# Block-causal attention and two MLP layers on one core: another table for the planner, with part of the normalization on GpSimd

## The chip, the cores and the metric

One Trainium2 chip, one core. The metric is the device time of one execution in microseconds (us). Engines are named as the profile names them: PE (TensorE, with PEld for its weight loads), DVE (VectorE), ACT (ScalarE), POOL (GpSimd), SP (SyncE, which issues nearly all DMAs).

## The reference

```python
# q, k, v: 4 batches x 8 heads x 576 tokens x 64
scores = 0.125 * q @ k.T
scores = np.where(block_i >= block_j, scores, -1e9)   # blocks of 64 tokens
attn = np.exp(scores - max(scores)); attn /= attn.sum(-1) + 1e-9
x = (attn @ v)                                        # as 2304 x 512
h = x @ w_in                                          # 512 x 2048
x = (s * np.maximum(h, 0)**2 + b) @ w_out             # 2048 x 512
h = max(x @ w1, x @ w2, x @ w3)                       # 512 x 768 each
out = h @ w_out2                                      # 768 x 512
```

The weights (`moe_w_in`, `moe_w_out`, `moe2_w*`) reach the kernel as pairs of 32-bit words and are taken apart on the chip.

## The kernel before, in words

Every product of the MLP layers is made of three fp32r matmuls on 128 rows and 128 columns (high by high, high by low, low by high part), so each operand exists as a high and a low part that ACT, DVE or POOL makes. Attention goes through 16 pairs of heads (`p` = 0 to 15). For a pair there are nine score units: units 1 to 8 cover 128 queries of one head each (192, 320, 448 or 576 keys; `unit`, line 573) and unit 0 the first 64 queries of both heads (`first`, line 546). DVE takes the row maximum out of PSUM (`most`, line 531), ACT the exponential with its row sum (`expo`, line 536). PE then transposes the exponentials in five groups a to e (`turned`, line 669), ACT or DVE copies them out, and PE multiplies them by the values (`product` A to E, line 672). The sums become reciprocals once a batch (four pairs), are turned, written to DRAM and read back over 64 partitions, and `normalize` (line 847) multiplies the result in `xf` by them, chunk by chunk (five chunks of 512 or 384 tokens); `split_x` (line 870) then makes high and low part of a chunk. The first three chunks go through the first half of the first MLP layer plainly, all that is left by Strassen's scheme with seven products. `convert` (line 745) makes float32 weights from those words.

PE works in three shapes. Scores and MLP use the array as one tile of 128 rows and 128 columns. The products A to E use two tiles of 128 rows and 64 columns side by side, one for each head (`side`), in plain fp32, for which the profile records two matmuls for each one in the code. Unit 0 also stands side by side, but contracts over 64 rows only, that is with tiles of 64 rows and 64 columns: two matmuls of 64 columns in the code, four records. `side_by_side` (line 698) collects what has been put on the list `side` and issues it as one block of PE work, in the order in which it was put there.

The order on every engine is computed when the program is built. Operations are recorded with the engines allowed, a cost in ns, what they read and write, and a due time (place in the recording plus `CFG['off']` of their kind); `Sched.run` (line 201) then fills the engines' in-order queues in model time. It holds POOL and those DVE operations that are marked `lock` to one at a time (`port`), and charges PE for going into and out of side-by-side blocks (line 261). It charges nothing for what stands inside such a block. 60 filler matmuls (kind `warm`, line 1142, 128x256) take PE's free places at the start. In what order the parts of a pair are recorded is a string:

```python
        for x in CFG["order%d" % p if p < 2 else "order"]:   # line 1248
```

A digit records that score unit (0 puts `first` on the list `side`), a small letter turns that group of the pair before, a capital puts that product of the pair before on `side`, `p` prepares the next pair's operands and loads those after, `v` loads values, and `|` issues the list as one block. Before, the string was

```python
        'order': '20DaEbC6|p75AB41||vd|ce3||8',
```

so its first block holds unit 0, then D, E and C.

For each pair the operands are made from `raw` tiles: high parts of keys and queries (`khi`, `qhi`), their low parts (`klo`, line 377 by a helper, and the query's on DVE, line 499) and `k0` for unit 0; `CFG['eng']` (and `eng0`, `eng1` for pairs 0 and 1) says on which engines. Pair 0 uses plain fp32 scores (tile `xf`) with one scaling operation `q2` of the queries ahead.

Of the kernel before, what the change touches and what calls it, by code (L numbers as in the profile page):

```python
# [29 lines left out]
EPS = 1e-9  # L30

# [33 lines left out]
def c_dve(n):  # L65
    return n / 0.96 + 68
# [22 lines left out]
def c_pooltt(n):  # L89
    return 2.4 * n + 100  # L90
# [64 lines left out]
class Sched:  # L155
# [45 lines left out]
    def run(self):  # L201
        n = len(self.ops)
# [25 lines left out]
        while len(order) < n:  # L228
# [28 lines left out]
            if e == "PE":  # L257

                m = self.ops[i][5]
                if side != (m == "side"):  # L260
                    c += 92 if not side else 126 if m == "turn" else 256
                side = m == "side"
# [20 lines left out]
def tile_attention_moe(ctx: ExitStack, tc: tile.TileContext, qk, vp, w_in, w_out, ms_, b_, w123, w_out2, out):  # L283
# [98 lines left out]
    def load(size, f, eng="SP", after=(), lat=2000, **k):  # L382

        k["after"] = [op(eng, 380, f, lat=lat, after=after, **k)]
        return op("DMA", size / (CFG["rate"] if k.get("kind") in ("w", "w2", "wf") else 330), lambda e: None, lat=1000 + CFG["dm"].get(k.get("kind"), 0), **k)
# [37 lines left out]
    def load_pair(p):  # L423
# [3 lines left out]
        if p == 0:  # L427

            for i, e_ in enumerate(("SP", "ACT")):
                def f(e, i=i):  # L430
                    (nc.sync if i == 0 else nc.scalar).dma_start(out=R[i].ap[0:64, 0:2 * S], in_=qk[b, hp, 0:64, i])
                load(294912, f, e_, lat=1260, writes=[(R[i], k) for k in ALL])
        else:
            for i in range(2):
                def f(e, i=i):
                    nc.sync.dma_start(out=R[i].ap, in_=qk[b, hp, :, i])
                load(589824, f, lat=2000 if p < 3 else CFG["dlat"], writes=[(R[i], k) for k in ALL])
# [75 lines left out]
    def load_values(p):  # L513
# [5 lines left out]
        load(557056, f, lat=2000 if p < 2 else CFG["dlat"], writes=[V])  # L519
        return V  # L520

    def softmax_pair(p, P, DEN):
# [86 lines left out]
    def values_pair(p, E, V):  # L609
# [7 lines left out]
        def turn(groups, u):  # L617
# [3 lines left out]
            for g in groups:  # L621
# [11 lines left out]
                op({x: y(n) for x, y in (("ACT", c_act), ("DVE", c_dve)) if x in CFG["pe"]}, 0, f,  # L633
# [213 lines left out]
    def normalize(c):  # L847
# [4 lines left out]
        for k in range(KT):  # L852
# [12 lines left out]
            op(CFG_E("xn", DVE=c_dve(n), Pool=c_pooltt(n)), 0, f, reads=[N] + [(XF, (k, i, tok)) for i in bs for tok in (0, 64)],  # L865
# [4 lines left out]
    def split_x(c, ring="x1"):  # L870
        c0, n = CHUNKS[c]
        for k in range(KT):
# [10 lines left out]
            j = op(CFG_E("xlo", DVE=c_dve(n), Pool=c_pooltt(n)), 0, f, reads=[(XF, ("x", c, k)), (X, 0)], writes=[(X, 1)], kind="xs", lock=True)  # L883
# [547 lines left out]
    with tc.manual_schedule():  # L1431
        for t, i, e in order:
# [4 lines left out]
CFG = {'aside': (6, 9, 12, 14, 18, 19, 23),  # L1437
        'aside3': (1, 1, 1, 0, 0, 0, 2, 0, 0, 2, 2, 0, 1, 1, 0, 2),
        'dlat': 5000,
        'dm': {'w': 1500, 'w2': 3300, 'wf': 2400},  # L1440
        'duo': (),
        'e': [2, 2, 2, 2, 2],
        'eng': {'k0': ['Pool', 'ACT', 'DVE'], 'khi': ['DVE'], 'klo': ['DVE', 'Pool'], 'q2': ['DVE', 'ACT', 'Pool'], 'qhi': ['DVE', 'Pool']},
        'eng0': {'k0': ['Pool', 'ACT'], 'khi': ['Pool', 'ACT', 'DVE'], 'klo': ['DVE'], 'q2': ['ACT'], 'qhi': ['Pool', 'DVE']},
        'eng1': {'k0': ['DVE'], 'khi': ['Pool', 'DVE', 'ACT'], 'klo': ['Pool', 'DVE'], 'q2': ['Pool', 'ACT'], 'qhi': ['ACT', 'Pool']},
        'ew': {'aff': ['ACT'],
               'hhi': ['DVE'],
# [9 lines left out]
        'je': ['ACT', 'DVE'],  # L1457
# [3 lines left out]
        'off': {'av': 625,  # L1461
                'exp': -7725,
                'h': -1300,
                'hf': -4560,
                'jc': -3650,
                'l1': -60,
                'l2': 40,
                'max': -6825,
                'phi': -1350,
                'prep': 125,  # L1470
                'prep0': -1000,
                'prep2': -350,
                'prepk': -2100,
                'prepklo': -7450,
                'preplo': -825,
                'smm': 175,
                'tr': -4875,
                'u': 260,
                'w': 940,
                'w0': -450,  # L1480
                'w2': 820,
                'warm': 1000000,
                'wf': -4620,
                'x2': -1160,
                'xn': 1340,
                'xs': 960},
# [70 lines left out]
```

## Time and profile before

| | |
|---|---|
| median of 3 runs | 822.62 us (822.43 to 823.08) |
| the profiled execution | 822.2 us |
| its span, first to last instruction | 820.4 us |
| PE busy | 814.6 us, 99% of the span, 4898 matmul records |
| DVE busy | 616.7 us, 75%, 1347 instructions |
| ACT busy | 479.3 us, 58%, 1100 instructions |
| POOL busy | 64.6 us, 8%, 57 instructions |
| granted TensorE clock, mean of the core | 1.000 |

Busy times of PE are modelled from the starts of its matmuls, so that a busy PE is not yet one at its peak: how fast it goes is read from how many matmuls start in a stretch. DVE and ACT have their load in attention (the first 160 us), where they are above 90% busy; later they have room.

### The profile page before, as it was taken

The numbers are of one execution on the slowest core, as the hardware profiler recorded it, in microseconds if no ns is written. First come the engines' busy times: TensorE is split into PE (matmuls) and PEld (weight loads), VectorE is DVE, ScalarE is ACT, GpSimd is POOL, SyncE is SP. The second block draws the span as 40 slices with busy tenths as digits, with TensorE's granted clock in tenths as the row PEclk, the third lists the DMA queues.
The fourth block names the chain that finished last, engine by engine and source line by source line (L and its number), as shares of the span: only waits on it lengthen the run. The fifth ranks groups of instructions, "written<-read, shape, count | busy, mean of one in ns | idle before, by whom it ended". The sixth has DMA issues, their size and how long they took to land. (4 is left out here: it accounts for less than half of the span.)

```text
span 820.4 us, 14499 instructions
## 1 busy us (share of the span) xinstructions
PE 814.6 (99%) x4898; PEld 741.4 (90%) x4898; DVE 616.7 (75%) x1347; ACT 479.3 (58%) x1100; POOL 64.6 (8%) x57
## 2 busy tenths in 40 slices
PE   9999999999999999999999999999999999999998
PEld 7778887878888899999999999999999899999996
DVE  7889999998778898879967997986557245833551
ACT  6888989986665688689666669622143122412111
POOL 5344254000000000000000000000000000000000
PEclk9999999999999999999999999999999999999999
DMA  7877786465678599899679799899676477666742
GB/s 236 256 253 210 230 275 208 177 192 198 228 262 305 211 302 354 307 353 376 203 271 323 259 319 338 291 306 306 212 232 206 142 228 229 181 194 188 225 128 77
DMA packets 92178, 200.77 MB, mean 245 GB/s; under 512 B 10948, under 2 KB 16452, under 8 KB 92100
## 3 DMA queue, kind: packets, MB, share of 16 engines
q1 hardware_dynamic: 91880, 199.41, 73.2%
q8 instruction: 39, 0.64, 0.3%
q10 hardware_dynamic: 224, 0.43, 0.2%
q14 instruction: 35, 0.29, 0.1%
HBM read 152.24 MB, written 43.85 MB: 239 GB/s over the span
## 5 line engine op out<-in xcount | busy, mean ns | idle before, releaser
L380 PE MATMUL ps<-arena 128*128 128x384 f32 (+4 forms) x3834 | 719.7, 347 | 1.4 <-DVE arena L1135 1.2
L380 PEld LDWEIGHTS ps<-arena 128*128 128x128 f32 x3834 | 668.9, 188 | 43.3 <-issue 1.4
L959 ACT ACTIVATE other<-ps 128x384 f32<-128x384 f32 x154 | 75.0, 487 | 186.8 <-PE ps L380 169.3
L954 DVE TENSOR_TENSOR other<-ps,other 128x384 f32<-128x384 f32 x129 | 71.2, 554 | 106.2 <-PE ps L380 90.0
L377 DVE TENSOR_TENSOR arena<-other,arena 128x384 fp32r<-128x384 f32 (+3 forms) x201 | 117.9, 598 | 5.2 <-ACT arena L364 2.3
L538 ACT ACTIVATE other<-ps,other 128x192 f32<-128x192 f32 (+4 forms) x144 | 77.7, 550 | 14.9 <-DVE other L533 14.5
L366 DVE TENSOR_SCALAR arena<-other 128x384 fp32r<-128x384 f32 (+3 forms) x148 | 60.2, 410 | 29.6 <-PE ps L380 19.7
L372 ACT ACTIVATE other<-ps 128x512 f32<-128x512 f32 (+1 forms) x102 | 55.8, 572 | 40.3 <-PE ps L380 36.2
L533 DVE TENSOR_REDUCE other<-ps 128x1 f32<-128x192 f32 (+4 forms) x144 | 66.9, 513 | 8.1 <-PE ps L380 7.3
L628 PEld LDWEIGHTS ps<-ident,other 128*128 128x128 f32 x400 | 43.9, 141 | 15.4 <-ACT other L538 10.7
L380 PE MATMUL ps<-other 128*64 128x64 f32 (+5 forms) x640 | 55.1, 313 | 0.0
L377 DVE TENSOR_TENSOR other<-other 128x256 fp32r<-128x256 f32 (+1 forms) x125 | 52.7, 433 | 1.6 <-ACT other L364 0.6
L760 ACT ACTIVATE other<-other 128x512 f32<-128x512 f32 x64 | 43.1, 676 | 17.8 <-DVE other L756 17.8
L628 PE MATMUL ps<-ident,other 128*128 128x128 f32 x400 | 53.4, 277 | 0.0
L768 DVE SCALAR_TENSOR_TENSOR other<-other 128x512 uint32<-128x512 uint32 x64 | 43.6, 687 | 6.7 <-ACT other L760 6.2
L364 ACT ACTIVATE other<-other 128x256 fp32r<-128x256 f32 (+2 forms) x95 | 39.0, 426 | 12.2 <-DMA bscr<-other 4.9
L1345 ACT ACTIVATE other<-other,cst 128x384 f32<-128x384 f32 x64 | 44.7, 701 | 0.7
L364 ACT ACTIVATE arena<-other 128x384 fp32r<-128x384 f32 (+1 forms) x66 | 36.4, 562 | 13.2 <-DVE other L377 10.2
L380 PEld LDWEIGHTS ps<-other 128*64 128x64 f32 (+1 forms) x640 | 26.9, 136 | 13.8 <-issue 9.7
L374 DVE COPY other<-ps 128x384 f32<-128x384 f32 (+2 forms) x49 | 28.2, 597 | 14.2 <-ACT other L372 11.9
L377 POOL TENSOR_TENSOR arena<-other,arena 64x1152 fp32r<-64x1152 f32 x11 | 37.8, 3436 | 11.9 <-PE ps L380 7.4
L1330 ACT ACTIVATE other<-other 128x384 f32<-128x384 f32 x48 | 24.8, 520 | 17.3 <-DVE other L954 17.2
(46 smaller groups left out, 426.7 us busy)
## 6 DMA issues: line engine op xcount, KB each, us to landing
arena<-bscr SPq DMA_DIRECT2D x301, 256.0 KB, 3.3
bscr<-other SPq DMA_DIRECT2D x119, 256.0 KB, 4.0
other<-qk SPq DMA_DIRECT2D x30, 576.0 KB, 5.1
other<-w_in SPq DMA_DIRECT2D x24, 512.0 KB, 5.0
other<-w_out SPq DMA_DIRECT2D x22, 512.0 KB, 5.4
other<-w SPq DMA_DIRECT2D x18, 512.0 KB, 6.1
other<-vp SPq DMA_DIRECT2D x16, 544.0 KB, 5.0
other<-pscr SPq DMA_DIRECT2D x24, 192.0 KB, 4.3
```

The lines of the kernel that those rows point to most:

```text
L364: nc.scalar.activation(out=dst, in_=src, func=AF.Copy, scale=m)
L366: nc.vector.tensor_scalar(out=dst, in0=src, scalar1=m, scalar2=None, op0=ALU.mult)
L372: nc.scalar.activation(out=dst, in_=src, func=AF.Copy)
L377: eng[e].tensor_tensor(out=dst, in0=a, in1=b, op=ALU.subtract)
L380: nc.tensor.matmul(o, l, r, start=start, stop=stop, **k)
L533: nc.vector.tensor_reduce(out=NM.ap[:, u:u + m], in_=v, axis=axis, op=ALU.max, negate=True)
L538: nc.scalar.activation(out=ev, in_=v, func=AF.Exp, bias=NM.ap[:, u:u + 1], scale=1.0, accum_out=DEN.ap[:, d:d + 1])
L628: nc.tensor.transpose(TB.ap[:, 128 * i:128 * i + 128], x, ident)
L768: nc.vector.scalar_tensor_tensor(out=lo_w, in0=hi_w, scalar=3, in1=lo_w, op0=ALU.logical_shift_left, op1=ALU.bitwise_or)
L954: nc.vector.tensor_tensor(out=out_.ap, in0=bank.ap[:, 0:HN], in1=u.ap, op=ALU.add)
L959: nc.scalar.activation(out=u.ap, in_=bank.ap[:, 0:HN], func=func)
L1345: nc.scalar.activation(out=u.ap, in_=u.ap, func=AF.Identity, scale=s_t, bias=b_t)
```

## The change

It changes numbers of the planner and its table, and where a few operations may run. In the planner: DVE's and ACT's copies of the transposes and the row maxima are charged 46 ns more (`EV`), two-operand work on POOL 2.7 instead of 2.4 ns a column, the ways into and out of side-by-side blocks 150, 216 and 290 instead of 92, 126 and 256 ns, loads of queries, keys and values other rates; weight loads are charged 1500 and 1600 ns less delay. In the kernel: the multiplications by the reciprocal sums of chunks 0 to 2 go to POOL, as does the low part of chunk 0 (`CFG['pool']`); the two units of 192 keys (i = 0) of a pair share a PSUM bank and one maximum (`duo`); high parts of hidden values may be made by ACT too; the result of a pair is copied out by DVE alone (`je`); `qhi` and `k0` go to ACT or POOL, `klo` to POOL. The strings and due times are others.

```diff
+EV = 46
 def c_pooltt(n):
-    return 2.4 * n + 100
+    return 2.7 * n + 100
...
-                    c += 92 if not side else 126 if m == "turn" else 256
+                    c += 150 if not side else 216 if m == "turn" else 290
...
-            op("DVE", c_dve(n), f, reads=reads, writes=[(NM, u + i) for i in range(m)], kind="max")
+            op("DVE", c_dve(n) + EV, f, reads=reads, writes=[(NM, u + i) for i in range(m)], kind="max")
...
-            op(CFG_E("xn", DVE=c_dve(n), Pool=c_pooltt(n)), 0, f, reads=[N] + [(XF, (k, i, tok)) for i in bs for tok in (0, 64)],
+            op({"Pool": c_pooltt(n)} if c < CFG["pool"][0] else CFG_E("xn", DVE=c_dve(n), Pool=c_pooltt(n)), 0, f, reads=[N] + [(XF, (k, i, tok)) for i in bs for tok in (0, 64)],
...
-            j = op(CFG_E("xlo", DVE=c_dve(n), Pool=c_pooltt(n)), 0, f, reads=[(XF, ("x", c, k)), (X, 0)], writes=[(X, 1)], kind="xs", lock=True)
+            j = op({"Pool": c_pooltt(n)} if c < CFG["pool"][1] else CFG_E("xlo", DVE=c_dve(n), Pool=c_pooltt(n)), 0, f,
+                   reads=[(XF, ("x", c, k)), (X, 0)], writes=[(X, 1)], kind="xs", lock=True)
...
-CFG = {'aside': (6, 9, 12, 14, 18, 19, 23),
-        'aside3': (1, 1, 1, 0, 0, 0, 2, 0, 0, 2, 2, 0, 1, 1, 0, 2),
+CFG = {'aside': (8, 11, 12, 14, 17, 18, 20),
+        'aside3': (2, 0, 0, 0, 1, 2, 0, 1, 3, 1, 0, 0, 0, 0, 0, 3),
-        'dm': {'w': 1500, 'w2': 3300, 'wf': 2400},
-        'duo': (),
+        'dm': {'w': 0, 'w2': 1700, 'wf': 2400},
+        'duo': (0,),
-        'eng': {'k0': ['Pool', 'ACT', 'DVE'], 'khi': ['DVE'], 'klo': ['DVE', 'Pool'], 'q2': ['DVE', 'ACT', 'Pool'], 'qhi': ['DVE', 'Pool']},
+        'eng': {'k0': ['ACT', 'Pool'], 'khi': ['DVE'], 'klo': ['Pool'], 'q2': ['Pool', 'DVE', 'ACT'], 'qhi': ['ACT', 'Pool']},
-        'eng0': {'k0': ['Pool', 'ACT'], 'khi': ['Pool', 'ACT', 'DVE'], 'klo': ['DVE'], 'q2': ['ACT'], 'qhi': ['Pool', 'DVE']},
+        'eng0': {'k0': ['Pool'], 'khi': ['ACT'], 'klo': ['Pool'], 'q2': ['DVE'], 'qhi': ['ACT']},
-               'hhi': ['DVE'],
+               'hhi': ['ACT', 'DVE'],
-        'je': ['ACT', 'DVE'],
+        'je': ['DVE'],
...
-        'order': '20DaEbC6|p75AB41||vd|ce3||8',
-        'order0': 'BpD3bc274Av5aC|6|8dE10e',
-        'order1': 'E0aA|D4618|bv5eCd||pB|c|3|72',
+        'order': 'CD20Ea|||vb6p74|5A1dB|e|||c3|8|',
+        'order0': 'p|av|EbC64e2cB37A|5|d81D0',
+        'order1': 'DaA2b0|p6||1B8||dE||5v7|e|c||C|3|4||',
+        'pool': (3, 1),
-        'pt': (1, 1, 2, 1, 1),
+        'pt': (1, 1, 1, 1, 1),
```

Where the changed kernel's instructions stand, at three places. First PE in one pair's cycle in the middle of attention: `arena` operands are scores, `ident,other` transposes, `other` alone the side-by-side products. Before:

```order
L380 MATMUL ps<-arena 128x320 x2
L380 MATMUL ps<-arena 128x288 x4
L380 MATMUL ps<-arena 128x192 x2
L380 MATMUL ps<-other 64x64 x2
L380 MATMUL ps<-other 64x128 x2
L380 MATMUL ps<-other 64x64 x10
L380 MATMUL ps<-other 64x256 x2
L628 MATMUL ps<-ident,other 128x128 x14
```

Now:

```order
L381 MATMUL ps<-arena 128x320 x2
L381 MATMUL ps<-arena 128x288 x4
L381 MATMUL ps<-arena 128x192 x4
L381 MATMUL ps<-other 64x256 x2
L381 MATMUL ps<-other 64x128 x2
L381 MATMUL ps<-other 64x64 x12
L629 MATMUL ps<-ident,other 128x128 x14
```

The block that holds unit 0 began with its two matmuls (64x64 x2). Now C (64x256) and D (64x128 and two of 64x64) come first, then unit 0 as the third and fourth of the twelve 64x64, then E. This follows from the string's `CD20E`, and is so for pairs 2 to 15. Over the whole program there are 33 side-by-side blocks before and now, with the same matmuls; 30 were followed by transposes and three by 128x128 matmuls, now 26 and seven; all 33 followed 128x128 matmuls, now 28 do and five follow transposes.

Second, PE at the start: `arena` 128x256 are the fillers, `xf` the scores of pair 0. Before:

```order
L380 MATMUL ps<-arena 128x256 x24
L380 MATMUL ps<-xf 128x192
L380 MATMUL ps<-arena 128x256 x5
L380 MATMUL ps<-xf 128x320
L380 MATMUL ps<-xf 128x288 x2
L380 MATMUL ps<-xf 128x320
L380 MATMUL ps<-xf 128x448 x2
L380 MATMUL ps<-xf 128x288 x2
L380 MATMUL ps<-xf 128x192
L380 MATMUL ps<-arena 128x256 x19
L628 MATMUL ps<-ident,other 128x128 x8
```

Now:

```order
L381 MATMUL ps<-arena 128x256 x29
L381 MATMUL ps<-xf 128x192 x2
L381 MATMUL ps<-xf 128x448
L381 MATMUL ps<-xf 128x320 x2
L381 MATMUL ps<-xf 128x288 x2
L381 MATMUL ps<-xf 128x448
L381 MATMUL ps<-xf 128x288 x2
L381 MATMUL ps<-arena 128x256 x14
L629 MATMUL ps<-ident,other 128x128 x14
L381 MATMUL ps<-arena 128x256 x17
L381 MATMUL ps<-other 64x64 x2
L381 MATMUL ps<-other 64x512 x2
```

The five fillers between the first and the second score matmul now stand ahead of the first, the scores run through, and 31 fillers follow them as before. The first side-by-side block holds unit 0 of pair 0, product A and, in the next row (64x64 x2), unit 0 of pair 1, where both units stood ahead of A. The 14 transposes are groups a and b of pair 0, and group a needs all eight exponentials.

Third, POOL in the later pairs, now: 64x1152 is `klo`, L865 the multiplication by the reciprocal sums, `arena<-xf` chunk 0's low part.

```order
L378 TENSOR_TENSOR arena<-other,arena 64x1152
L369 TENSOR_SCALAR other<-other 64x128
L865 TENSOR_TENSOR xf<-xf,other 128x512 x2
L378 TENSOR_TENSOR arena<-xf,arena 128x512
L378 TENSOR_TENSOR arena<-other,arena 64x1152
L378 TENSOR_TENSOR arena<-xf,arena 128x512
L865 TENSOR_TENSOR xf<-xf,other 128x512
L378 TENSOR_TENSOR arena<-other,arena 64x1152
```

Before, one `klo` of 64x1152 and one `qhi` of 128x1024 stood here for a pair, and none of the other rows; three of the 14 `klo` were on DVE. Now all 14 stand on POOL with 12 multiplications and four low parts between them, and three `qhi` are left.

## Rows read from the trace of the kernel before

**Rows 1.** The page: the span, and busy time by engine (share, instructions).
```profile
span 820.4 us, 14499 instructions
PE 814.6 (99%) x4898; PEld 741.4 (90%) x4898; DVE 616.7 (75%) x1347; ACT 479.3 (58%) x1100; POOL 64.6 (8%) x57
```
**Rows 2.** Who waited for whom, PE: us in total, times, longest.
```profile
PE ps L380 <- DVE arena L1135: 1.2, 1, 1.2
...
PE ps L380 <- DVE other L1415: 0.3, 1, 0.3
```
**Rows 3.** Stretches: length, then PE, PEld, DVE, ACT, POOL; clock, DMA, GB/s.
```profile
40.00:80.00 40.00, 40.00 (x361) 31.04 (x358) 36.20 (x69) 34.93 (x111) 16.97 (x12) 1.00 0.76 237
80.00:120.00 40.00, 40.00 (x385) 31.76 (x384) 38.93 (x71) 36.48 (x114) 15.41 (x14) 1.00 0.78 246
120.00:160.00 40.00, 40.00 (x362) 31.87 (x361) 39.20 (x82) 36.19 (x106) 13.01 (x7) 1.00 0.66 210
...
360.00:400.00 40.00, 40.00 (x232) 39.98 (x231) 37.44 (x87) 35.15 (x75) 0.00 (x0) 1.00 0.89 321
```
**Rows 4.** PE in order of time, one pair: start, length, engine, line, form, records.
```profile
62.17 1.72 PE L380 MATMUL ps<-other 64*64 64x64 f32 x32
63.82 1.75 PE L628 MATMUL ps<-ident,other 128*128 128x128 f32 x14
...
71.41 0.81 PE L380 MATMUL ps<-other 64*64 64x64 f32 x11
```
**Rows 5.** PE in order of time, the last pair's block of C, D and E.
```profile
154.73 1.45 PE L380 MATMUL ps<-other 128*64 128x128 f32 x28
156.11 2.95 PE L628 MATMUL ps<-ident,other 128*128 128x128 f32 x25
```
**Rows 6.** PE in order of time, 72 MLP matmuls behind a transpose, behind a block.
```profile
161.70 16.61 PE L380 MATMUL ps<-arena 128*128 128x512 f32 x72
...
179.89 16.66 PE L380 MATMUL ps<-arena 128*128 128x512 f32 x72
```
**Rows 7.** PE in order of time, the start.
```profile
1.18 4.44 PE L380 MATMUL ps<-arena 128*128 128x256 f32 x24 [1.18 <-DVE arena L1135]
6.34 0.56 PE L380 MATMUL ps<-xf 128*128 128x192 f32 x2 [0.71 <-issue]
6.60 0.89 PE L380 MATMUL ps<-arena 128*128 128x256 f32 x5
7.33 5.07 PE L380 MATMUL ps<-xf 128*128 128x320 f32 x18
12.10 2.56 PE L380 MATMUL ps<-arena 128*128 128x256 f32 x19
14.51 1.26 PE L628 MATMUL ps<-ident,other 128*128 128x128 f32 x8
```
**Rows 8.** ACT in order of time: scaling of queries, last exponential of pair 0.
```profile
5.82 0.42 ACT L364 ACTIVATE xf<-xf 64x256 f32<-64x256 f32 x1 [1.18 <-DMA xf<-qk]
...
14.85 0.20 ACT L538 ACTIVATION_READ_ACCUMULATOR other<-ps,other 128x1 f32 x1
```
**Rows 9.** POOL in order of time: two `klo` of the same size.
```profile
28.65 2.64 POOL L377 TENSOR_TENSOR arena<-other,arena 64x1152 fp32r<-64x1152 f32 x1 [3.47 <-DVE arena L366]
...
36.17 3.62 POOL L377 TENSOR_TENSOR arena<-other,arena 64x1152 fp32r<-64x1152 f32 x1 [1.04 <-DVE arena L366]
```
**Rows 10.** DVE in order of time, beside the second of them.
```profile
36.06 1.22 DVE L499 SCALAR_TENSOR_TENSOR arena<-other,arena 64x1024 fp32r<-64x1024 f32 x1
```
**Rows 11.** DVE groups by form: count, busy us, mean ns, idle before them.
```profile
L756 DVE TENSOR_SCALAR other<-other 128x512 f32<-128x512 f32 x64 | 27.0, 421 | 3.4 <-DMA other<-w_in 2.5 <-DMA other<-w_out 0.8
...
L864 DVE TENSOR_TENSOR xf<-xf,other 128x512 f32<-128x512 f32 x12 | 8.2, 685 | 0.1
L377 DVE TENSOR_TENSOR arena<-xf,arena 128x512 fp32r<-128x512 f32 x12 | 7.9, 677 | 0.1
...
L374 DVE COPY xf<-ps 128x512 f32<-128x512 f32 x3 | 2.1, 685 | 0.2 <-PE ps L380 0.2
...
L374 DVE COPY xf<-ps 128x64 f32<-128x64 f32 x3 | 0.6, 216 | 0.0
```

More of the change, by code (lines that the diff above doesn't have):

```diff
@@ L380, in mm, with load @@
         nc.tensor.matmul(o, l, r, start=start, stop=stop, **k)
-    def load(size, f, eng="SP", after=(), lat=2000, **k):
+    def load(size, f, eng="SP", after=(), lat=2000, rate=330, **k):
         k["after"] = [op(eng, 380, f, lat=lat, after=after, **k)]
-        return op("DMA", size / (CFG["rate"] if k.get("kind") in ("w", "w2", "wf") else 330), lambda e: None, lat=1000 + CFG["dm"].get(k.get("kind"), 0), **k)
+        return op("DMA", size / (CFG["rate"] if k.get("kind") in ("w", "w2", "wf") else rate), lambda e: None, lat=1000 + CFG["dm"].get(k.get("kind"), 0), **k)
     def CFG_E(k, **c):
@@ L431, in f @@
                     (nc.sync if i == 0 else nc.scalar).dma_start(out=R[i].ap[0:64, 0:2 * S], in_=qk[b, hp, 0:64, i])
-                load(294912, f, e_, lat=1260, writes=[(R[i], k) for k in ALL])
+                load(294912, f, e_, lat=1260, rate=240, writes=[(R[i], k) for k in ALL])
         else:
@@ L436, in f @@
                     nc.sync.dma_start(out=R[i].ap, in_=qk[b, hp, :, i])
-                load(589824, f, lat=2000 if p < 3 else CFG["dlat"], writes=[(R[i], k) for k in ALL])
+                load(589824, f, rate=400, lat=2000 if p < 3 else CFG["dlat"], writes=[(R[i], k) for k in ALL])
         return R
@@ L518, in f @@
             nc.sync.dma_start(out=V.ap, in_=vp[b, hp])
-        load(557056, f, lat=2000 if p < 2 else CFG["dlat"], writes=[V])
+        load(557056, f, rate=400, lat=2000 if p < 2 else CFG["dlat"], writes=[V])
         return V
@@ L632, in f @@
                     copy_to(e, PT.ap[:, o], TB.ap[:, 0:n])
-                op({x: y(n) for x, y in (("ACT", c_act), ("DVE", c_dve)) if x in CFG["pe"]}, 0, f,
+                op({x: y(n) + EV for x, y in (("ACT", c_act), ("DVE", c_dve)) if x in CFG["pe"]}, 0, f,
                         reads=[TB], writes=[(PT, c)], kind="phi")
@@ L1460 @@
         'nmx': 4,
[L1461 to L1465, printed above, removed]
+        'off': {'av': 1550,
+                'exp': -7000,
+                'h': -1640,
+                'hf': -5660,
+                'jc': -4325,
                 'l1': -60,
[L1467 to L1468 removed]
+                'l2': 140,
+                'max': -10325,
                 'phi': -1350,
[L1470 to L1481, printed above, removed]
[L1482 to L1489 removed]
+                'prep': 2225,
+                'prep0': 900,
+                'prep2': -1800,
+                'prepk': -3025,
+                'prepklo': -7175,
+                'preplo': -1325,
+                'smm': 1250,
+                'tr': -5200,
+                'u': -960,
+                'w': 1120,
+                'w0': -175,
+                'w2': 940,
+                'warm': 1000000,
+                'wf': -4160,
+                'x2': -1520,
+                'xn': 1520,
+                'xs': 560},
+        'order': 'CD20Ea|||vb6p74|5A1dB|e|||c3|8|',
+        'order0': 'p|av|EbC64e2cB37A|5|d81D0',
+        'order1': 'DaA2b0|p6||1B8||dE||5v7|e|c||C|3|4||',
         'pe': ['ACT', 'DVE'],
         'ph': 0,
[L1492 removed]
+        'pool': (3, 1),
+        'pre': (0, 0, 0, 0, 0, 1, 0, 0, 0, 0, 0, 0, 0, 1, 1, 0, 0),
         'psb': {'av': [7], 's': [0, 1, 2, 3, 4, 5, 6], 's2': [0, 1, 2, 3, 4, 5, 6], 't': [0, 1, 2, 3, 4, 5, 6]},
[L1494 removed]
+        'pt': (1, 1, 1, 1, 1),
         'q2d': 2,
```

3 lines of the change are left out of this document (1 added, 2 removed).

## The prediction

> **What bounds the kernel now.** The page comes first: PE is busy for 814.6 of 820.4 us [rows 1]. That figure is modelled, so it says only where to look. The view of who waited for whom has next to nothing for PE: 1.2 us for the memset that its fillers read, and 0.3 us at one place late in the MLP layers [rows 2]. The table by stretches then shows whether PE goes at its pace. In the MLP stretch from 360 to 400 us 232 matmuls of 384 columns start in 40 us, one every 0.172 us, at a granted clock of 1.00, with DVE busy for 37.44 and ACT for 35.15 of 40 us beside it [rows 3]. In attention DVE is busy for 36.20, 38.93 and 39.20 of 40 us and ACT for 34.93 to 36.48 [rows 3], yet the view of waits names no PE wait there [rows 2]. So the kernel is one PE queue without holes, and two numbers decide: how long PE's own queue takes, and whether another engine opens a hole. The number and form of the matmuls don't change. What can change is the cost of going from one tile shape to another, the few holes at the start, and new holes.
>
> The attention view shows the cycle: from one block of 32 records (unit 0, D, E, C) to the next 71.41 − 62.17 = 9.24 us [rows 4], all of it PE work.
>
> **The change, part by part.**
>
> *Unit 0 in the middle of its block.* Unit 0 contracts over 64 rows, its neighbours over 128. The block with it lasts from 62.17 to 63.82, 1.65 us [rows 4]; the last pair's block of D, E and C without it from 154.73 to 156.11, 1.38 us [rows 5]. Both come behind scores and end in transposes, so the 0.27 us between them is unit 0 in full. Its four records have 4 × 64 = 256 columns. The 28 records without it have 4 × 128 + 20 × 64 + 4 × 256 = 2816 columns in 1.38 us, so 256 columns at that pace are 0.125 us. The other 0.145 us is no streaming: it is what the one change from 64-row to 128-row tiles costs. Before, unit 0 came first, and the way into the block covered the other direction. Now C and D stand ahead and E behind, so the block goes 128, 64, 128 rows: one change more in each of 14 blocks (pairs 2 to 15), and one more in the first block, where A stands between the two units. The trace has no change from 128 to 64 rows inside a block. From below I bound it by 0, from above by all of unit 0's cost, 0.27 us. The nearest row is the same pair of shapes in the other direction, so I take 0.145: 15 × 0.145 = 2.2 us, all on PE's path (0 to 4.0 us).
>
> The Trainium skill, "TensorEngine Tiling (Array Packing)", section "Key Properties", says that changing the tiling mode, as against moving to another tile of the same mode, drains TensorE. By that sentence the change costs in both directions and the sum stays at 2.2 us; by the rows alone the unseen direction could be free. The trace agrees for 64 to 128 rows (0.145 us), and nothing before shows the way back.
>
> *Ways out of and into blocks.* Seven blocks instead of three now go straight back to 128x128 matmuls rather than to transposes. 72 matmuls of 512 columns take 16.61 us behind a transpose and 16.66 us behind a block [rows 6]: 4 × 0.05 = 0.2 us. Five blocks now follow transposes, which the trace doesn't show; I take 0, between plus and minus the change of shape, 5 × 0.145 = 0.7 us either way.
>
> *The start.* PE's first score starts at 6.34 us after 0.71 us without work; its fillers were spent [rows 7]. It waited for ACT's scaling, 5.82 + 0.42 = 6.24 us [rows 8]. Five more fillers now stand there. A filler takes (14.51 − 12.10) / 19 = 0.127 us [rows 7], so they cover 0.63 of the 0.71 us, and the five between the first and second score (7.33 − 6.60 = 0.73 us) are gone. The scores end 0.73 us earlier. Behind them 31 fillers stand as before. That gives 0.6 us, if pair 0's last exponential (14.85 + 0.20 = 15.05 us before [rows 8]) comes earlier too: ACT is rid of the scalings (0.42 us for the first), but gets another high part. If it doesn't, the 14 transposes, now due from about 13.2 us, wait for it and the gain is gone. I take −0.6, between −1.0 and +0.3 us.
>
> *DVE, ACT and POOL.* DVE loses 12 multiplications (8.2 us) and four low parts (4 × 0.677 = 2.7 us) and gets 13 more pairs of copies of the result (13 × (0.685 + 0.216) = 11.7 us) [rows 11]; fewer maxima and three fewer `klo` go with it. It stays about as full as it is. ACT gives up those copies and gets most of the query's high parts from POOL; in attention it has 120 − 107.6 = 12.4 us of 120 us free [rows 3]. I cost both at nothing: cover is PE's queue, as before. If that cover fails, PE waits (second rival).
>
> *POOL's queue.* A `klo` took 2.64 us alone and 3.62 us where DVE's two-operand operation (1.22 us from 36.06) was running at its start [rows 9, 10]. So 1152 columns cost 2.64 us, and 512 some 512/1152 of it, 1.17 us. The 12 multiplications and four low parts are 18.7 us on an engine with 45 us of work in 120 us [rows 3]. Next in POOL's queue behind a multiplication is a `klo`, for which the next pair's scores wait. With three added operations to a pair POOL has 3.62 + 3 × 1.17 = 7.1 us and a `k0` in a cycle of 9.4 us. I cost it at 0.
>
> *Weights.* The planner now counts on weights 1.5 us earlier, so their conversions stand earlier in DVE's queue. DVE stood idle 3.4 us in all for such a load [rows 11]. Double that is 3.4 us on an engine with room; on PE I put 0, at most 3.4 us. MLP matmuls run at their pace [rows 3], so nothing is to be had there but the 0.3 us [rows 2].
>
> Sum: +2.2 + 0.2 − 0.6 = **+1.8 us**. The profiled execution took 822.2 us for a span of 820.4 us, so it would be 824.0 us; it stands 0.4 us below the median, 822.62 us. Forecast for the median: **824.4 us**.
>
> **The rivals.**
>
> *The way back is free.* If 128 to 64 rows costs nothing, 2.2 us fall away: 822.62 + 0.2 − 0.6 = 822.2 us, no difference. For it: no row shows that direction. Against it: the other direction between the same shapes has its 0.145 us [rows 4, 5], and nothing in the code sets the two apart.
>
> *POOL holds DVE up, slower still.* That the longer `klo` is longer by about the overlap with DVE's operation [rows 9, 10] says that such operations take turns. If each of the 16 added ones keeps DVE from its next two-operand operation for 1.17 us, that is 18.7 us on an engine with 120 − 114.3 = 5.7 us free in 120 us [rows 3]; DVE's row maxima stand behind, and PE's transposes behind those. If a fifth comes through to PE, 3.7 us more: 828.1 us. It decides where DVE's backlog in a pair passes what PE has queued. Against it: 11 `klo` of over twice the length did this before without a wait of PE [rows 2]. The Trainium skill, "GPSIMD Engine Reference", section "Key points", says that GpSimd shares its SBUF interfaces with VectorE and contends with its two-input and two-port operations; the two `klo` agree, 2.64 and 3.62 us.
>
> *Faster.* If the way back is free, the start gives its 1.0 us, the five blocks behind transposes save 0.7 us, and late waits of some 0.5 us go (the 0.3 us [rows 2] and smaller ones): 822.62 − 2.2 = 820.4 us. It needs all of this together.
>
> **How the numbers follow.** About 0.2%, 1.64 us, is what a measurement here can tell from no change: faster is below 820.98, slower above 824.26 us. The forecast's own mechanism gets 0.48, with a range of its own from 823.3 to 825.6 us, because the change of shape is measured in one direction and the gain at the start depends on one exponential; 0.18 of it lies within the 0.2%, 0.30 above. The free way back gets 0.22 (0.19 same, 0.03 faster), POOL against DVE 0.20 (slower), the sum of gains 0.10 (0.06 faster, 0.04 same). Together: faster 0.09, same 0.41, slower 0.50. The range from 821.3 to 828.0 us leaves out most of the last case and the upper half of the POOL case.
>
> **What would show it.** In the new profile a block with unit 0 lasts 1.65 + 0.145 = 1.80 us from its start to the transposes, and a cycle 9.39 instead of 9.24 us; PE's waits stay short in attention. The first score starts near 6.3 us right behind 29 fillers, and pair 0's transposes near 13.2 instead of 14.51 us [rows 7], without a hole inside them. If blocks last 1.65 us, the first rival holds. If PE's waits name DVE or POOL, or `klo` ends late in pairs with multiplications, the second does. A cycle of 9.24 us or less would make the prediction wrong, as would holes in the MLP layers that answer to weights.

## The result, and the profile after

The changed kernel takes **828.9 us** (median of 4 runs, 828.52 to 830.09) against 822.75 us for the kernel before beside it (4 runs): ratio 1.0076, 95% interval 1.0063 to 1.009. It is 6.2 us slower; 1.8 us had been forecast, and the time lies 0.9 us above the range's upper end. The profiled execution took 828.94 us.

The page after, to be read against [rows 1]: the span, busy time by engine, and the shares of the chain that ended last.

```profile
span 827.2 us, 14439 instructions
PE 820.2 (99%) x4898; PEld 745.5 (90%) x4898; DVE 600.6 (73%) x1268; ACT 510.1 (62%) x1154; POOL 81.4 (10%) x66
...
PE 92%; DVE 5%; ACT 2%; issue 1%; DVEq 0%; ACTq 0%
```

DVE has lost 16 us of work and POOL gained 17, and yet DVE now stands on the chain. Who waited for whom, PE of the kernel after (engine, line, waited for: us in total, times, longest), where before there were two waits for another engine [rows 2] and 0.7 us at the first score [rows 7]:

```profile
PE ps L381 <- DVE arena L1137: 1.2, 1, 1.2
PE ps L723 <- DVE other L718: 0.4, 1, 0.4
PE ps L381 <- DVE other L1417: 0.4, 1, 0.4
PE ps L381 <- ACT other L373: 0.4, 1, 0.4
PE ps L381 <- DVE arena L378: 0.4, 1, 0.4
PE ps L381 <- ACT other L1016: 0.2, 1, 0.2
PE ps L381 <- DVE xf L375: 0.2, 1, 0.2
```

The first is again the memset at the start. The others have become many and short, each for an operation of DVE, or of ACT. The stretches after (columns as in [rows 3]) show that this isn't a matter of load:

```profile
40.00:80.00 40.00, 40.00 (x355) 31.04 (x355) 35.60 (x67) 35.38 (x107) 18.46 (x13) 1.00 0.78 234
80.00:120.00 40.00, 39.55 (x353) 31.02 (x350) 36.14 (x62) 36.99 (x109) 24.73 (x17) 1.00 0.83 248
120.00:160.00 40.00, 40.00 (x374) 31.34 (x374) 36.77 (x68) 36.32 (x106) 15.57 (x9) 1.00 0.71 229
```

DVE is busy for 108.5 us of these 120, where it was for 114.3 [rows 3]. DVE has more room and PE waits for it more: what counts is when an operation ends, not how many there are. PE in order of time shows the pair cycle, to be set beside [rows 4]:

```profile
63.57 1.86 PE L381 MATMUL ps<-other 128*64 128x256 f32 x32
65.36 1.75 PE L629 MATMUL ps<-ident,other 128*128 128x128 f32 x14
...
72.97 1.86 PE L381 MATMUL ps<-other 128*64 128x256 f32 x32
74.76 1.75 PE L629 MATMUL ps<-ident,other 128*128 128x128 f32 x14
```

The block with unit 0 in its middle lasts 74.76 − 72.97 = 1.79 us, 0.15 more than before, and the cycle 72.97 − 63.57 = 9.40 instead of 9.24 us. The waits that the view names are only part of what PE loses. I took the time from the start of each PE record to the start of the next, and subtracted the lower quartile of that time for the same two forms in the profiles shown. Remainders of over 0.03 us are called holes below; they add up so (us):

| stretch of PE's queue | before | after |
|---|---|---|
| first side-by-side work, to 21 us | 0.3 | 0.5 |
| attention to 158 us | 1.3 | 1.9 |
| end of attention (last pair's products) | 0.0 | 1.5 |
| plain MLP, to 320 us | 0.3 | 1.3 |
| Strassen, first layer | 0.6 | 0.1 |
| second layer, from 555 us | 0.6 | 1.6 |
| all | 3.1 | 6.9 |

So the kernel after has 3.8 us more of holes. With 15 × 0.147 = 2.2 us for the blocks (next section) this is 6.0 of the 6.7 us between the two profiled executions; where the other 0.7 us are, the count doesn't show.

### The profile page after: what moved, and what is told of

Read it like the earlier page. It is cut to its first block, busy times and chain, and to the rows that moved or that the text cites. A ratio compares the mean times of both kernels' runs of the same rounds, so it can differ in the third digit from the quotient of the medians.

```text
span 827.2 us, 14439 instructions
## 1 busy us (share of the span) xinstructions
PE 820.2 (99%) x4898; PEld 745.5 (90%) x4898; DVE 600.6 (73%) x1268; ACT 510.1 (62%) x1154; POOL 81.4 (10%) x66
## 4 chain that ended last, share of the span: by engine, by line
PE 92%; DVE 5%; ACT 2%; issue 1%; DVEq 0%; ACTq 0%
PE ps L381 87%; PE ps L629 5%; DVE arena L378 1%; DVE other L769 1%; DVE arena L500 1%; DVE other L534 0%; ACT other L761 0%; DVE other L765 0%; ACT other L1016 0%; ACT other L1028 0%; ACT other L1021 0%; DVE other L757 0%; DVE other L375 0%; DVE other L956 0%; ACT arena L365 0%
## 5 line engine op out<-in xcount | busy, mean ns | idle before, releaser
L381 PE MATMUL ps<-arena 128*128 128x384 f32 (+3 forms) x3834 | 722.3, 348 | 2.5 <-DVE arena L1137 1.2
L365 ACT ACTIVATE arena<-other 128x384 fp32r<-128x384 f32 (+3 forms) x158 | 91.0, 588 | 74.7 <-PE ps L381 54.5
L378 DVE TENSOR_TENSOR arena<-other,arena 128x384 fp32r<-128x384 f32 (+2 forms) x197 | 113.8, 592 | 27.5 <-ACT arena L365 25.4
L539 ACT ACTIVATE other<-ps,other 128x448 f32<-128x448 f32 (+4 forms) x144 | 77.8, 550 | 6.8 <-DVE other L534 6.5
L373 ACT ACTIVATE other<-ps 128x512 f32<-128x512 f32 (+2 forms) x105 | 56.2, 557 | 39.6 <-PE ps L381 31.8
L534 DVE TENSOR_REDUCE other<-ps 128x1 f32<-128x320 f32 (+4 forms) x128 | 67.4, 560 | 12.5 <-PE ps L381 11.2
L378 POOL TENSOR_TENSOR arena<-other,arena 64x1152 fp32r<-64x1152 f32 (+1 forms) x15 | 44.9, 2992 | 23.0 <-PE ps L381 14.4
L367 DVE TENSOR_SCALAR arena<-other 128x384 fp32r<-128x384 f32 (+2 forms) x67 | 30.6, 457 | 16.0 <-PE ps L381 10.1
L375 DVE COPY other<-ps 128x512 f32<-128x512 f32 (+2 forms) x46 | 28.4, 625 | 16.5 <-ACT other L373 11.9
L1340 ACT ACTIVATE other<-other 128x384 f32<-128x384 f32 x64 | 32.9, 518 | 0.5
```

The source lines that it names most:

```text
L365: nc.scalar.activation(out=dst, in_=src, func=AF.Copy, scale=m)
L373: nc.scalar.activation(out=dst, in_=src, func=AF.Copy)
L378: eng[e].tensor_tensor(out=dst, in0=a, in1=b, op=ALU.subtract)
L381: nc.tensor.matmul(o, l, r, start=start, stop=stop, **k)
L539: nc.scalar.activation(out=ev, in_=v, func=AF.Exp, bias=NM.ap[:, u:u + 1], scale=1.0, accum_out=DEN.ap[:, d:d + 1])
```

## The experiments

Times are medians; the kernel before took 822.5 to 822.9 us beside them.

### Where unit 0 stands

**e2**, the kernel before with unit 0 (its function marked `unit0` in `first`) put behind the block's first two products, and nothing else:

```diff
-            def f(e, fs=[x[1] for x in side]):
+            own, rest = ([x[1] for x in side if hasattr(x[1], "unit0") == u] for u in (True, False))
+            mixed = own[:1] + rest + own[1:] if len(own) > 1 else rest[:2] + own + rest[2:]
+            def f(e, fs=mixed):
```

> The kernel before with the same plan on every engine; unit 0 stands between products in its block, as in the changed kernel (30 changes instead of 15). Theory: 15 x 0.147 = 2.2 us more than before, 825.0 us. Rival (a change from 128 to 64 rows is free): as before, 822.8 us.

824.98 us, ratio 1.0028 (1.0017 to 1.0039): +2.2 us. **e3**, the kernel before with unit 0 over 128 rows (lower rows zero, written once by DVE), so that no block changes its tile:

```diff
-k0=Strip(other, K0AT, 256, lambda t: t[0:64])
+k0=Strip(other, K0AT, 256)
...
+            nc.vector.memset(other.tile[64:128, at0:at0 + 256], 0.0)
```

> The kernel before; unit 0 contracts over 128 rows, the lower 64 of both operands being zeros that two VectorE memsets write once, so that its tiles have the shape of its neighbours' and no change of tile rows is left (0 instead of 15). Theory (the cost is the change of shape): 15 x 0.147 = 2.2 us less than before, 820.5 us. Rival (the cost is unit 0's own, its weights or its PSUM bank): as before, 822.8 us.

821.1 us, ratio 0.9981 (0.9973 to 0.999): −1.65 us where 2.2 had been expected, and faster than both kernels. PE in order of time, first e2, then e3:

```profile
73.31 1.86 PE L380 MATMUL ps<-other 128*64 128x128 f32 x32
75.10 1.75 PE L629 MATMUL ps<-ident,other 128*128 128x128 f32 x14
```

```profile
71.08 1.57 PE L380 MATMUL ps<-other 128*64 128x64 f32 x32
72.58 1.75 PE L628 MATMUL ps<-ident,other 128*128 128x128 f32 x14
```

The same 32 records take 1.79 us with two changes inside the block, 1.65 with one [rows 4], 1.50 with none: about 0.147 us a change, in either direction. By the Trainium skill, "TensorEngine Tiling (Array Packing)", "Key Properties", a change of tiling mode drains TensorE; these blocks agree.

The same two edits in the changed kernel: **e1** puts unit 0 first again (the list sorted), **e4** takes the 128 rows.

> The changed kernel with the same plan on every engine; only inside the side-by-side blocks unit 0 stands ahead of C, D, E again (16 changes between 64-row and 128-row tiles instead of 30). Theory (each change of tile rows costs TensorE 0.147 us in either direction): blocks with unit 0 go from 1.79 back to 1.65 us, 14 x 0.147 = 2.1 us less than the changed kernel, so 826.8 us, still 4.0 us above before. Rival (the longer blocks only filled time in which PE would have waited anyway, or 128 to 64 rows is free): blocks shorter, but the time stays at 828.9 us, since PE then waits longer elsewhere.

> The changed kernel with unit 0 over 128 rows as in e3 (0 changes of tile rows instead of 30). Theory: 30 x 0.147 = 4.4 us less than the changed kernel, 824.5 us, so that what it still stands above e3 (about 4 us) is not the shape of the tiles but waits. Rival (the shorter blocks turn into waits): between 826 and 829 us.

e1: 827.82 us (−1.1 instead of −2.1); e4: 827.89 us (−1.0 instead of −4.4). Both differences are hardly clear of the noise: the five runs of e1 go from 827.12 to 828.69, those of e4 from 826.25, the profiled one, to 829.4 us. That e4 falls short of 4.4 us is clear. The blocks are shorter as planned, but holes in attention grow from 1.9 to 3.0 (e1) and 3.9 us (e4). Waits of PE in e4, beside the list of the kernel after:

```profile
PE ps L723 <- DVE other L718: 0.7, 1, 0.7
PE ps L381 <- DVE arena L378: 0.7, 1, 0.7
...
PE ps L381 <- DVE xf L375: 0.4, 2, 0.2
```

In the changed order attention is held by DVE's and ACT's order as well as by PE: a PE that is through sooner meets the same operations earlier, and waits for them.

### The multiplications on GpSimd

**e5** leaves out the twelve multiplications of chunks 0 to 2 (these chunks stay unnormalized, so it does less work); **e6** issues them and chunk 0's four low parts on DVE where POOL had them; **e8** does the reverse to the kernel before; **e10** gives all 16 to DVE before the order is computed. The edits of the multiplications:

```diff
 e5: +                if c >= 3:
 e6: -                eng[e].tensor_tensor(...)
     +                eng["DVE"].tensor_tensor(...)
     ...
 e8: +                eng["Pool" if c < 3 else e].tensor_tensor(...)
     ...
 e10: -        'pool': (3, 1),
      +        'pool': (0, 0),
```

> The changed kernel, same plan, without the 12 multiplications by the reciprocal sums on GpSimd (chunks 0 to 2 stay unnormalized; their loads of the sums stay). Theory A (GpSimd's multiplications hold VectorE out of the port they share, and PE waits for what stands behind): the holds at 80, 95, 150 and 159 us go, with them PE's waits at 99.9 us (0.6 us) and at 162 to 165 us (1.4 us): 2 us less, 826.9 us. Rival B (the waits come from the table: what stands ahead of the waiting work in VectorE's and ScalarE's queues): under 0.5 us less, 828.4 us or more.

> The changed kernel, same plan, but the 12 multiplications and the first chunk's four low parts are issued on VectorE at the places that they had in time (11 us more work there, none of the 16 on GpSimd). Theory A: VectorE is held less but works more, so waits of PE stay about as they are: 827 to 830 us. If it is faster than the kernel without any multiplication, A falls; if it is 2 us slower than the changed kernel, the move to GpSimd is worth something in this plan.

> The kernel before, same plan, with the named part of the change alone: the 12 multiplications of chunks 0 to 2 and the four low parts of chunk 0 are issued on GpSimd at the places that they had on VectorE. Theory A: each holds VectorE for up to 1.27 us, and what GpSimd makes next (query high parts, key low parts) comes later: 0.5 to 2 us more than before, 823.3 to 824.8 us. Rival B: VectorE is relieved of 11 us and has slack: no more than 822.9 us.

> The changed kernel with the twelve multiplications and four low parts given back to DVE before the order is computed, so that the plan knows of them (in the run with them moved to DVE at their old places it did not). Theory (their place on POOL costs about 2 us): 826.9 us, no holes at the end of attention. Rival (on DVE they push its other work back and PE waits elsewhere): 828 us or more.

| | us | ratio to before | difference |
|---|---|---|---|
| e5 | 826.73 | 1.0048 (1.0036 to 1.0061) | −2.2 to after |
| e6 | 828.14 | 1.0067 (1.0053 to 1.0081) | −0.8 to after |
| e8 | 824.63 | 1.0022 (1.0012 to 1.0032) | +1.8 to before |
| e10 | 825.55 | 1.0032 (1.0019 to 1.0044) | −3.4 to after |

So the multiplications on POOL cost about 2 us in either kernel: against leaving them out in the changed one (e5), against DVE's places in the one before (e8). Issued on DVE at POOL's places they take 0.8 us less, hardly clear of the noise (e6; its interval overlaps that of the kernel after). The 3.4 us of e10, more than its theory gave, are what the plan gains by knowing the work on DVE, and they include what else a new order brings. How POOL's part comes about is seen in the changed kernel at the end of attention, all engines in order of time:

```profile
159.02 2.70 POOL L865 TENSOR_TENSOR xf<-xf,other 128x512 f32<-128x512 f32 x2 [5.19 <-DMA other<-scr]
159.37 1.21 DVE L765 TENSOR_SCALAR other<-other 128x512 uint32<-128x512 uint32 x1
...
159.90 2.95 PE L629 MATMUL ps<-ident,other 128*128 128x128 f32 x25
...
160.50 1.50 DVE L757 TENSOR_SCALAR other<-other 128x512 f32<-128x512 f32 x1
...
162.04 0.69 ACT L761 ACTIVATE other<-other 128x512 f32<-128x512 f32 x1 [1.72 <-DVE other L757]
162.62 0.58 ACT L373 ACTIVATE other<-ps 128x512 f32<-128x512 f32 x1
162.65 0.42 DVE L757 TENSOR_SCALAR other<-other 128x512 f32<-128x512 f32 x1
...
163.26 2.65 PE L381 MATMUL ps<-other 128*64 128x512 f32 x8 [0.41 <-ACT other L373]
```

POOL's two multiplications run from 159.02 to 161.72. Two steps in the conversion of a weight that has nothing to do with them, 0.42 us each by themselves (the row at 162.65), take 1.21 and 1.50 us beside them. ACT waits 1.72 us for the second of them; its copy of the last pair's transposes stands behind that conversion in its queue, and PE waits for the copy. DVE's own copies of those transposes stand behind the conversions too, and the block at 163.26, eight records, lasts 2.65 us with the waits inside it; the same block lasts 1.73 us in e5. The Trainium skill, "GPSIMD Engine Reference", "Key points", names contention on the shared SBUF interfaces for DVE's two-input operations and those in a two-port mode; L757 has one tensor input, so by that sentence it would be of the second sort. The trace agrees that it is held up: 1.50 us instead of 0.42. The stretch around it, eight us each, columns as in [rows 3], in the kernel after, in e5 and in e10:

```profile
158.00:166.00 8.00, 7.59 (x67) 5.05 (x66) 7.76 (x14) 5.60 (x13) 2.70 (x2) 1.00 0.04 12
```

```profile
158.00:166.00 8.00, 8.00 (x72) 5.99 (x71) 7.92 (x19) 6.34 (x14) 0.00 (x0) 1.00 0.02 7
```

```profile
157.00:165.00 8.00, 8.00 (x73) 5.98 (x72) 7.93 (x19) 5.96 (x14) 0.00 (x0) 1.00 0.30 101
```

Without POOL's work DVE gets 19 operations through instead of 14, and PE has no wait there. In e8 the same thing happens to another operation, later: POOL's multiplication of 1.37 us starts at 177.38 us, and a low part on DVE, 0.69 us by itself, takes until 179.30:

```profile
177.51 1.79 DVE L377 TENSOR_TENSOR arena<-other,arena 128x512 fp32r<-128x512 f32 x1
```

ACT then waits 1.82 us for DVE's next conversions, and PE 0.38 us for ACT and 0.33 us for DVE, which end at 181.6 and 182.7 us.

e6 gains less than e5 in part because DVE, with the multiplications in its own queue, reaches the reciprocal (L718) later still: the hole at 100 us grows from 0.6 to 1.15 us. In the kernel after that hole follows a `klo`, not a multiplication, and it stays in e5:

```profile
93.30 2.64 POOL L378 TENSOR_TENSOR arena<-other,arena 64x1152 fp32r<-64x1152 f32 x1 [3.55 <-PE ps L381]
...
95.04 1.99 DVE L500 SCALAR_TENSOR_TENSOR arena<-other,arena 64x1024 fp32r<-64x1024 f32 x1
...
100.10 0.38 DVE L718 RECIPROCAL other<-other 128x36 f32<-128x36 f32 x1
```

The operation at 95.04, of a form that takes 1.22 us where nothing holds it up [rows 10], is 0.77 us longer, and DVE has no gap from there to the reciprocal.

**e7** puts one `klo`, pair 2's, on DVE, since it holds DVE up ahead of the wait at 19.5 us (0.5 us):

```diff
-                sub_to(e, kl[0:64], k[0:64], f32(kh[0:64]))
+                sub_to("DVE" if p == 2 else e, kl[0:64], k[0:64], f32(kh[0:64]))
```

> The changed kernel, same plan, but the low part of pair 2's keys (64x1152), which GpSimd makes at 14.5 us and which holds VectorE's two-operand work for pair 1, is made by VectorE at that place (1.3 us). Theory A: PE's wait at 19.5 us (0.54 us, up to 0.9 us in the runs with shorter blocks) goes or becomes 0.5 us or less: 828.4 us, within the noise of this kernel, so the trace has to show it. Rival: VectorE is only busy by itself there, and the wait stays or grows.

831.47 us (828.82 to 833.36), ratio 1.0105 (1.009 to 1.012). The wait at 19.5 us is gone, and two others come, which end at 99.9 and 102.05 us. Most of the profiled run's loss is something else, below under the hardware.

### Taking several costs away together

**e13**: 128 rows, no multiplications, one weight conversion moved. **e14**: the same with multiplications on DVE. **e18**: e10 and 128 rows.

> The changed kernel with unit 0 over 128 rows (30 changes of tile rows gone, 30 x 0.147 = 4.4 us), without the twelve multiplications by the reciprocal sums (chunks 0 to 2 stay unnormalized, so this run does less work), and with the conversion moved as in the run before. If the three parts add up: 828.9 - 4.4 - 2.2 - 0.8 = 821.5 us, and PE's holes in attention stay at 1.9 us. Rival (attention is also bound by other engines now, so that shorter blocks turn into waits even without the multiplications): holes in attention 3.5 us or more, 823.5 us or more.

> As the run before, but with the twelve multiplications and chunk 0's low parts computed, on DVE at the places where POOL had them. If parts add up: 828.9 - 4.4 - 0.8 (what moving them to DVE gave) - 0.8 = 822.9 us. Rival (DVE has no room in attention, shorter blocks turn into waits): holes in attention 4 us or more, 825.5 us or more.

> The changed kernel with the multiplications and low parts planned on DVE (825.55 us by itself) and unit 0 over 128 rows, so that all 30 changes of tile rows are gone (30 x 0.147 = 4.4 us). If both add up: 821.2 us, faster than the kernel before. Rival (shorter blocks turn into waits for DVE, as they did with POOL's multiplications): 823.5 us or more, and holes in attention of 4 us or more instead of 2.2 us.

e13 826.52, e14 826.71, e18 824.12 us (ratio 1.0015, 1.0006 to 1.0024): the rivals' times, with holes in attention of 3.3, 4.4 and 3.0 us (in e13 and e18 fewer than the rivals named). The moved conversion in e13 and e14 gained nothing by itself (e9, below: +0.7 by the medians). e18 keeps 1.4 of 4.4 us, and the changed plan without its two shown costs still isn't below the kernel before.

### The second layer, the charges, the start

**e9** (after) moves one conversion of the second layer's weights earlier, **e17** gives the kernel before the changed kernel's row for them:

```diff
 e9: -        'aside3': (2, 0, 0, 0, 1, 2, 0, 1, 3, 1, 0, 0, 0, 0, 0, 3),
     +        'aside3': (2, 0, 0, 0, 1, 2, 0, 1, 3, 1, 0, 0, 1, 0, 0, 2),
 e17: -        'aside3': (1, 1, 1, 0, 0, 0, 2, 0, 0, 2, 2, 0, 1, 1, 0, 2),
      +        'aside3': (2, 0, 0, 0, 1, 2, 0, 1, 3, 1, 0, 0, 0, 0, 0, 3),
```

> One conversion of the second layer's weights stands four Strassen steps earlier in the changed kernel, nothing else of the order of work differs up to the Strassen stage. The changed kernel (828.9 us) has 1.6 us of PE holes behind 555 us, the kernel before 0.6 us; the largest, 0.60 us at 565.7 us, ends with a sum on DVE that stands behind conversions. Theory (late conversions make this second-layer part of the loss): those holes shrink by 0.6 to 1.0 us, 828.1 us. Rival (DVE's queue is what it is there, and another wait comes in its place): 828.9 us, holes still 1.4 us or more.

> The kernel before with one row of the changed table alone: at which Strassen steps the second layer's weights are converted. Attention and its order stay as they were. Theory (this row brings the waits behind 555 us: 1.6 us of holes in the changed kernel, 0.6 us before): 823.5 us, and holes of about 1.6 us there. Rival (those waits come from other entries of the table): 822.7 us, holes of 0.6 us.

e9 (the conversion moved by three steps, not four): 829.64 us, ratio 1.0087 (1.0073 to 1.01), holes there 2.6 us; e17: 822.94 us, ratio 1.0002 (0.9993 to 1.001), holes 0.8 us. The theory fell twice: that row by itself isn't what brings the 1.0 us. What does stays open.

**e11**: the changed kernel's charges with the table before, multiplications on DVE.

> The changed kernel's planner charges with the table of the kernel before, and multiplications and low parts on DVE; unit 0 stands first in its block, so 16 changes of tile rows as before. Theory (the loss comes from the table's order and from POOL's multiplications, not from the charges): 822.8 us, within 0.8 us. Rival (the charges place DVE's and ACT's operations so that PE waits): PE's holes over 5 us instead of 3.1, 825 us or more.

842.03 us (ratio 1.0236, 1.0222 to 1.025), where 822.8 had been expected. PE's longest entries among its waits in e11:

```profile
PE ps L629 <- ACT other L539: 5.6, 6, 2.4
PE ps L723 <- DVE other L718: 2.1, 1, 2.1
```

PE waits for exponentials. Another part of the loss is TensorE's clock (last section). Charges and table belong together in this kernel: the one without the other costs 19.5 us, most likely because the due times of the table had been set with its own charges.

**e15** moves only the five fillers of the start in the kernel before, **e16** does so with e3. The edit takes them from behind the first score and puts them ahead of it, once the order is computed:

```diff
     order = sch.run()
+    late = pe[one + 1:two_]
+    order = [x for x in order if x not in late]
+    at = order.index(pe[one])
+    order[at:at] = late
```

> The kernel before with one thing of the changed kernel's start: the five fillers between the first and the second score stand ahead of the first. In five profiles with the old order of the start the first side-by-side block began 17.77 to 18.91 us after the span's start (mean 18.35), in nine with the changed one at 16.79 to 17.91 us (mean 17.26). Theory (those five fillers cover a hole and stand no longer in the way, as the forecast's step on the start has it): the block begins 0.6 to 1.1 us earlier, 822.0 us. Rival (the gain comes from the order of the transposes behind the scores, or the moved fillers push the first score back while the clock is still low): no gain, 822.6 us or more.

> The kernel before with unit 0 over 128 rows (821.1 us by itself) and with the five fillers ahead of the first score. If both add up: 820.4 us, the fastest of the study. Rival (earlier starts turn into waits for DVE or ACT): 821.1 us.

822.87 us (ratio 0.9998, 0.9989 to 1.0007) and 821.21 us: nothing gained. e15 in order of time:

```profile
6.79 0.56 PE L380 MATMUL ps<-xf 128*128 128x192 f32 x2 [0.58 <-issue]
6.79 0.83 ACT L364 ACTIVATE xf<-xf 64x768 f32<-64x768 f32 x1
...
7.76 1.02 PE L380 MATMUL ps<-xf 128*128 128x320 f32 x3 [0.41 <-ACT xf L364]
```

The second score waits for ACT's second scaling, which ends at 6.79 + 0.83 = 7.62 us. In the kernel before the five fillers stood in that wait and cost nothing.

## Why the prediction was wrong

**Unit 0 in the middle of its block** (+2.2): right, in size and in cause. 0.147 us a block against 0.145 forecast, and e2 gives 2.2 us alone. The rival of a free way back falls.

**POOL's queue** (0): the step that failed. It asked whether POOL would be late for the next scores, and named an average load; no wait of PE names POOL, so it wasn't late. It set down nothing for what POOL does to DVE while it works, which the second rival did: a fifth of 18.7 us, 3.7 us, 828.1 us in all. Measured were 2.2 (e5), 1.8 (e8) and 3.4 us with a new order (e10), so that rival was right in its first link, and its 3.7 us are up to twice the measured cost. Its second link was not right: at the end of attention it isn't row maxima and transposes, but a weight conversion with one input, through ACT and through DVE's own queue, into the copies of the transposes. That 828.1 us is near the measured 828.9 is in part luck, since the rival had none of the new waits below. The rival had been given 0.20 because eleven longer `klo` did no harm before. The rows say why they didn't: nine of the eleven began just after an operation of DVE, as in [rows 9, 10], and it was POOL's that grew, to 3.55 to 3.65 us, while DVE's kept its 1.22 us. In the kernel after, five DVE operations that began while a multiplication was running took 3.9 us longer in all (six in e8, 5.3 us). In these traces, of two that got in each other's way, the one that began second was the longer. "It decides where DVE's backlog in a pair passes what PE has queued": at the end of attention PE has little queued. Now the last pair's first block (163.26 us) comes straight behind its transposes, and 36 matmuls of 512 columns (24 and 12) lie between it and the next block. Before, 84 (12 and 72) lay ahead of the first block and 72 between the two [rows 6]. That gap in the cover costs nothing by itself: e5 has the same order and no wait there.

**DVE and ACT** (0): DVE became less busy and yet holes came that end with its operations, so the average was no cover.

**Ways out of blocks** (+0.2) **and blocks behind transposes** (0): not tried by themselves; neither is shown.

**The start** (−0.6, between −1.0 and +0.3): right in direction, too small, and its reason isn't borne out. The first side-by-side block begins 1.1 us earlier on average (18.3 us in seven profiles with the start before, e15 and e16 among them, 17.2 in eleven with the changed one). In the order before, moving the fillers gains nothing (e15). What is left of the start's change, DVE making the scalings and the two units of 192 keys sharing a maximum, wasn't tried apart. In the changed kernel's own profile the block is at 17.63 us against 17.77 in the profile before, because its clock rose late (last section).

**Weights** (0, at most 3.4): right. DVE's first step of the conversions (L757) stood idle 2.1 us in all for loads, 3.4 us before [rows 11], and no wait of PE follows from it. Other holes came: 1.0 us more in the plain MLP, of which e5 takes 0.6 and e10 all, and 1.0 us in the second layer, not settled.

Put together: −1.1 (start) + 2.2 (blocks) + 3.4 (e10: POOL's part, the plain MLP's holes with it) + 1.0 (second layer) + 0.5 (the wait at 19.5 us) = 6.0 us of 6.2. Of the 3.4 us about 2 are POOL's work by itself (e5, e8); the rest came with the order that e10 computed anew, and its causes weren't separated. So the sum missed about 2 us for POOL, shown, and about 3 us that came with the new order otherwise (1.4 + 1.0 + 0.5), seen in the traces as waits for DVE and ACT but not each explained; the forecast's answer to such waits was "cover is PE's queue, as before". The range took in POOL's case only in its lower half.

## What to carry to other kernels

Where an order is tuned until one engine has no holes, the others' slack is a matter of places, not of averages: a new operation is to be costed at each place by what it lengthens on the other engine, and by who stands behind that in order. Work on GpSimd isn't free for being off the path; here it lengthened the DVE operations that began while it ran, and the shortest chain from there to PE passed through a third engine's queue. And a gain on the bounding engine is worth what it was forecast only as long as nobody waits next: the 0.147 us a change came through for three quarters in the kernel before (e3, 1.65 of 2.2 us) and for about a quarter in the changed one (e4, by its median).

## What the hardware showed besides

TensorE's clock at the start rises at a time that isn't the kernel's. The fillers go from 213 to 118 ns, the granted clock from its lower level, 1.2 GHz, to 2.4 GHz, at 4.1 to 7.3 us over all the profiles here. With fillers ahead of the first score a late rise pushes that score back: kernel after first, where 29 fillers take 6.12 us, e15 second, where the same 29 take 5.02 us.

```profile
1.18 6.12 PE L381 MATMUL ps<-arena 128*128 128x256 f32 x29 [1.18 <-DVE arena L1137]
7.14 1.19 PE L381 MATMUL ps<-xf 128*128 128x192 f32 x5
```

```profile
1.18 5.02 PE L380 MATMUL ps<-arena 128*128 128x256 f32 x29 [1.18 <-DVE arena L1135]
```

Short waits stood ahead of a fall of the clock. In e7 PE waited 0.66 us ahead of four transposes at 99.91 us and 1.48 us behind them, and from 103 us on the granted clock stood at the lower level (PE in order of time, then stretches):

```profile
99.91 0.66 PE L629 MATMUL ps<-ident,other 128*128 128x128 f32 x4 [0.66 <-ACT other L539]
102.05 0.27 PE L723 MATMUL ps<-ident,other 128*36 128x128 f32 x1 [1.48 <-DVE other L718]
```

```profile
103.00:109.00 6.00, 6.00 (x47) 5.10 (x46) 3.22 (x7) 3.73 (x11) 3.57 (x2) 0.50 0.38 79
109.00:110.00 1.00, 1.00 (x8) 1.00 (x7) 0.69 (x1) 0.40 (x3) 0.00 (x0) 0.65 0.95 378
110.00:111.00 1.00, 1.00 (x9) 0.97 (x8) 0.43 (x1) 1.00 (x3) 0.00 (x0) 1.00 1.02 281
```

From that L723 on, the same ten scores, one block of 32 records and 14 transposes take 109.88 − 102.05 = 7.83 us in e7 and 105.39 − 100.63 = 4.76 us in the kernel after: 3.1 us more, beside 2.1 us for the waits themselves. It goes with the spread of e7's runs: 828.82 us at a mean clock of 1.000, 833.36 us, this profile, at 0.995. e11's profile shows it too: the granted clock stood at the lower level from 111.3 to 118.2 us and from 121.6 to 125.0 us, the first fall inside a wait of PE of 2.42 us, the second behind one of 2.06 us. 14 transposes take 3.02 us there, from 114.86 us on, and 1.50 us at full clock, from 95.94 us on. All five runs of e11 have a mean clock of 0.993 to 0.995, so part of its loss is the clock. What such a fall takes is left open.
